# Cluster masks for routed attention: from TensorE products to VectorE writes into the scores' PSUM banks, in the last seven pairs of heads

## The chip, the cores and the metric

The kernel runs on one core of a Trainium2 chip. The metric is the device time of one execution in microseconds. The engines are TensorE (PE in the profile, its weight loads PEld), VectorE (DVE), ScalarE (ACT), GpSimd (POOL) and the queue that issues DMAs (SP). Each engine works through its own queue of instructions in order and waits for others by semaphores.

## The reference

Routed attention over 4 batches of 8 heads, 768 positions and head size 64, and behind it a feed-forward network (FFN) with hard-swish. Each query and each key is assigned to one of 16 clusters of its head, and a query sees only the keys of its own cluster:

```python
q_assign = np.argmax(np.einsum('bhsd,hcd->bhsc', q_n, c_n), axis=-1)
k_assign = np.argmax(np.einsum('bhsd,hcd->bhsc', k_n, c_n), axis=-1)
mask = q_assign[:, :, :, None] == k_assign[:, :, None, :]
scores = scale * np.matmul(q, k.transpose(0, 1, 3, 2))
scores = np.where(mask, scores, -1000000000.0)
attn = np.exp(scores - np.max(scores, axis=-1, keepdims=True))
attn = attn / (np.sum(attn, axis=-1, keepdims=True) + 1e-09)
x = np.matmul(attn, v)          # then reshaped to 3072 tokens x 512
h = x @ w_in                    # 512 -> 2048
y = (h * np.clip(h + 3.0, 0.0, 6.0) / 6.0) @ w_out
```

(q_n, k_n and c_n are the unit vectors.)

## The kernel before

Heads are worked in 16 pairs of two (t = 0, 1 in the code), g = 0 to 15. A pair has 12 steps: two halves of 384 queries (hf) times six blocks of 128 keys (j). Step n of 192 makes one tile of scores for both heads, keys on the partitions: `ps`, 128 x 2 x 384 in two PSUM banks, out of a pool of two such tiles. Per step:

- `scores`: two mask products and two score products on TensorE, summed in PSUM. The score product takes the turned q and k (`xf`, fp32, 64 rows per head; each is two instructions in the profile). The mask product takes the turned one-hot cluster vectors (`xm`, bf16, made by `route` and `route_turn`), those of the keys inverted and scaled by -2^60, so that every pair in different clusters gets a huge negative score.
- `exponentials`: ScalarE reads `ps` and writes `ex` (six buffers). This frees the `ps` tile for step n + 2.
- `key_sums`: GpSimd adds `ex` into `acc`.
- `attn_v`: TensorE multiplies `ex` with v into `pv`, six steps to a half; ScalarE copies it to `num`.
- `divide`: two products with ones turn `acc` into denominators `pd`; VectorE takes the reciprocal and multiplies `num`.

The order of all instructions is written out by hand (`manual_schedule`): the program's order is each engine's order. From step 96 on (pair 8, `DECODED`), the loop over n goes in double steps and `four_by_four` groups two of them. With r = n mod 12:

- At r = 0, 4, 8: scores of n and n + 1, exponentials, and then `attn_v` of the four steps before.
- At r = 2, 6, 10: scores of n and n + 1, exponentials, and after them FFN items out of the list `fill`, with the preparation of the next pair (`prep_items`) between them: turning q and k at r = 2, the routing at r = 6, `route_turn` at r = 10. Then the next double step's scores follow at once in TensorE's queue.

The count of FFN items per group of four steps comes from `items_by`, 53 items to 48 steps, so 4 or 5. One block of the FFN is 8 up items and 7 down items. An up item (`halved`) is 14 products in the two PSUM tiles uX and uY. VectorE works in three parts on it: a copy and two adds after uX, three adds after uY, and a clip, which `finish` defers by one item (the last up item of a block does two). A down item is 8 or 16 products, with adds on VectorE after parts 1, 3 and 6 only. `token_sums` (four adds) stand in part 4. Items of both kinds share one PSUM pool of two tiles (`psum_m`).

The kernel also holds a second way to mask, unused before, as `MASKED = NPAIR` exceeds every g: `clusters` makes cluster numbers instead of one-hot vectors, `spread` broadcasts those of the queries over the partitions by 12 products per pair, and `masks` multiplies `ex` by a comparison on VectorE after the exponential.

Of the kernel before, what the change touches and what calls it, by code (L numbers as in the profile page):

```python
# [17 lines left out]
C = 16  # L18
P = 128
# [97 lines left out]
def fast_path(ctx, tc, ok, q, k, v, centroids, moe_w_in, moe_w_out, out):  # L117
# [48 lines left out]
    counts = const.tile([P, 2, NPAIR], F32, name="counts")  # L166
    w_low = const.tile([P, 1], F32, name="w_low")

    MASKED = NPAIR
    st = {}  # L170
    later = []
    numbers = []
# [87 lines left out]
    cen = startp.tile([P, D], F32, name="cen")  # L260
    parity = const.tile([P, 2], F32, name="parity")

    number = const.tile([P, C], BF16, name="number")

    def constants():
        make_identity(nc, ident)
        for t in range(2):
            nc.vector.tensor_reduce(
                out=parity[:, t : t + 1],
                in_=ident.rearrange("p (h t c) -> p t h c", t=2, c=C)[:, t], axis=AX.XY, op=ALU.max,  # L270
            )
        nc.gpsimd.memset(half_c, 0.5)
        nc.gpsimd.memset(low_c, 1.0 / BOUND)
        nc.gpsimd.memset(ones, 1.0)
        nc.gpsimd.memset(w_low, W_LOW)
        nc.gpsimd.memset(one_hot, 0.0)
        for c in range(C):
            nc.gpsimd.memset(number[:, c : c + 1], float(c))

        warm = psum_t.tile([P, 4, P], F32, name="warm", tag="t")  # L280
        for i in range(14):
            nc.tensor.transpose(out=warm[:, i % 4], in_=ident, identity=ident)
# [47 lines left out]
    def route(g):  # L330
        cs = st.pop(("cs", g))
        pr = scratch([P, NC2, 2, C], "pr")
        for i in range(NC2 // 4):
            nc.tensor.transpose(out=pr[:, 4 * i : 4 * i + 4], in_=cs[:, i], identity=ident)
        pr = pr.rearrange("p j t c -> p (j t) c")
        mx = rtp.tile([P, 2 * NC2], F32, name="mx")
        nc.vector.reduce_max(out=mx, in_=pr, axis=AX.X)
        oh = one_hot.rearrange("p j (t c) -> p j t c", t=2)[:, :, :, 0:C]
        pr = pr.rearrange("p (j t) c -> p j t c", t=2)
        mx = mx.rearrange("p (j t) -> p j t", t=2)  # L340
        halves = [slice(0, NCH), slice(NCH, NC2)]
# [14 lines left out]

        later.append(count)
        if g >= MASKED:
            numbers.append(lambda: clusters(g))

    def route_turn(g, part):
        if part == 0:
# [11 lines left out]
        return where(n)[0] >= MASKED  # L374

    def clusters(g):
        oh = one_hot.rearrange("p j (t c) -> p j t c", t=2)[:, :, :, 0:C]
        which = rtp.tile([P, NC2, 2, C], BF16, name="which")
        nc.vector.tensor_tensor(
            out=which, in0=oh, in1=number.unsqueeze(1).unsqueeze(1).to_broadcast([P, NC2, 2, C]), op=ALU.mult  # L380
        )
        qid = st["qid"] = rtp.tile([P, NCH, 2], BF16, name="qid")
        kid = st["kid", g] = kidp.tile([P, NCH, 2], F32, name="kid")
        nc.vector.tensor_reduce(out=kid, in_=which[:, NCH:], axis=AX.X, op=ALU.add)

        nc.vector.tensor_scalar(
            out=kid, in0=kid, scalar1=-1.0, scalar2=C * (C - 1) / 2.0, op0=ALU.mult, op1=ALU.add
        )
        qsum = rtp.tile([P, NCH, 2], F32, name="qsum")
        nc.vector.tensor_reduce(out=qsum, in_=which[:, 0:NCH], axis=AX.X, op=ALU.add)  # L390
        nc.vector.tensor_copy(out=qid, in_=qsum)

    def spread(g, part):
        if part == 0:
# [14 lines left out]

    def scores_qk(n):  # L410
        st["ps", n] = psum_s.tile([P, 2, 512], F32, name="ps")
        scores_part(n, st["xf", where(n)[0]], True, by_vector(n))

    def scores_part(n, x, first, last):
        g, hf, j = where(n)
        for t in range(2):
            r = slice(t * D, (t + 1) * D)
            nc.tensor.matmul(  # L418
                st["ps", n][:, t, 0:HALF], lhsT=x[r, NCH + j],
                rhs=x[r, hf * NHC : (hf + 1) * NHC], start=first, stop=last,  # L420
            )

    def scores(n):
        g, hf, j = where(n)
        if ("ps", n) not in st:
            if hf == j == 0 or by_vector(n):
                scores_qk(n)
            else:  # L430
                st["ps", n] = psum_s.tile([P, 2, 512], F32, name="ps")
                scores_part(n, st["xm", g], True, False)
                scores_part(n, st["xf", g], False, True)
                return
        if not by_vector(n):
            scores_part(n, st["xm", g], False, True)

    def exponentials(n):
        sc = st.pop(("ps", n))[:, :, 0:HALF]
        ex = st["ex", n] = expp.tile([P, 2, HALF], F32, name="ex")  # L440
        nc.scalar.activation(out=ex, in_=sc, func=ACT.Exp, scale=SM_SCALE)  # L441

    def masks(n):
        g, hf, j = where(n)
        if not by_vector(n):
            return
        ex = st["ex", n]
        for t in range(2):
            nc.vector.scalar_tensor_tensor(
                out=ex[:, t].rearrange("p (a b) -> p a b", b=P),  # L450
                in0=st["xm", g][:, t * NCH + hf * NHC : t * NCH + (hf + 1) * NHC],
                scalar=st["kid", g][:, j, t : t + 1], in1=ex[:, t].rearrange("p (a b) -> p a b", b=P),
                op0=ALU.is_equal, op1=ALU.mult,
            )

    def key_sums(n):
# [27 lines left out]


    def divide(n):
        g, hf, _ = where(n)
# [10 lines left out]
        rcp = nump.tile([P, HALF], F32, name="rcp")  # L498
        nc.vector.reciprocal(out=rcp, in_=pd)  # L499
        nc.vector.tensor_tensor(out=num, in0=num, in1=rcp, op=ALU.mult)  # L500

        def keep():
            nc.sync.dma_start(st["xd", b][:, kt, hf * HALF : (hf + 1) * HALF], num)
            in_range(2 * g + hf, rcp)
            if (kt, hf) == (NKT - 1, 1):
                later.append(lambda: (waiting.extend((b, m) for m in range(NHC)), load_block()))

        return keep


    def in_range(i, rcp):
# [278 lines left out]

    st["early"] = st["free"] = True
    st["last"] = False
    fill, checks, unmasked = [], [], []
    st["done"], st["valued"] = 0, DECODED - lag_v

    def check_all():
# [8 lines left out]
    def four_by_four(n, r, steps):  # L805
        for i in steps:
            scores(i)
        if r % 4 == 2:
            for i in steps:
                exponentials(i)  # L810
            unmasked.extend(steps)
            check_all()
            for op in numbers:
                op()
            numbers.clear()
            return


        for i in steps[: 1 if r == 8 else 2]:
            exponentials(i)  # L820
        check_all()
        for i in unmasked:
            masks(i)
            key_sums(i)
        unmasked.clear()
        if r == 4 or n >= total:
            m = n - r % per_pair - 1 if n < total else total - 1
            if ("acc", *where(m)[:2]) in st and m < st["valued"]:
                later.append(divide(m))
                ready(m)  # L830
        for i in range(st["valued"], min(n, total)):
            attn_v(i)
            if i % per_pair == NCH - 1:
                later.append(divide(i))
        st["valued"] = min(n, total)
        for i in steps[1 if r == 8 else 2 :]:
            exponentials(i)
        for i in steps:
            masks(i)
            key_sums(i)  # L840

    with tc.manual_schedule():
        nc.scalar.dma_start(cen, centroids.rearrange("h c d -> (h c) d"))
# [17 lines left out]
        for n in range(0, total + lag_d + 2, 2):  # L861
# [25 lines left out]
            if not fours or r % 4 == 2 or n >= total:  # L887
                want = min(items_by(n + 2) - st["done"], len(fill))
                st["done"] += want
                for i in range(max(len(prep), want)):  # L890
                    if i < want:
                        fill.pop(0)()
                    if i < len(prep):
                        prep[i]()
            if r == 6 and fours:
                load(g + 2, "q", "k")
                load(g + 1, "v")
# [403 lines left out]
```

## Time and profile before

| | |
|---|---|
| time, median of 3 (lowest to highest) | 1015.35 us (1015.34 to 1015.49) |
| span of the profiled execution | 1013.6 us |
| granted TensorE clock | 0.999 |
| score products, `ps<-xf` | 768 rows, mean 487 ns, 157.1 us |
| mask products, `ps<-xm` | 384 rows, mean 327 ns, 61.0 us |
| exponentials, ACT `ex<-ps` | 192, mean 805 ns |
| reciprocal, DVE `rcp<-pd` | 32, mean 2554 ns |
| clip, DVE `g_sb<-sx,g_sb` | 88, mean 770 ns |
| turning the one-hots, PE `po` and ACT `xm<-po` | 192 of mean 220 ns, 32 of mean 806 ns |

How to read it: a row's mean is the time of one instruction from its start to its end. Matmuls are pipelined, so the mean is longer than what one adds to TensorE's queue; that has to be read as the distance from start to start in the timeline. A line of the timeline shows the start, the time until the group's end, the engine, the line, what is written and read, the shape and the count, and in brackets idle time before it with the one that ended it. The window of the last seven pairs (9 to 15) is 308 to 766 us after the span's start.

### The profile page before, as it was taken

The page shows a single profiled execution, that of the slowest core. Times are in us where ns is not written, and L with a number is a line of the kernel's source. Part 1 is how long each engine was busy: PE and PEld are TensorE (multiplying, and loading weights), DVE is VectorE, ACT ScalarE, POOL GpSimd, SP SyncE. Part 2 cuts the span into 40 slices and gives each one's busy share as a digit, 9 for nine tenths or more (in the row PEclk, how much of TensorE's full clock was granted, in tenths as well). Part 3 has the DMA queues.
Part 4 walks back from the last instruction along what each step waited for, and adds up shares of the span by engine and source line. Part 5 has one row for each costly group of instructions (what it writes and reads, how often), then busy time and mean ns, then how long its engine had stood idle before and what let it go on. Part 6 is the DMA issues. An engine that isn't in the chain of part 4 may idle for free.

```text
span 1013.6 us, 16743 instructions
## 1 busy us (share of the span) xinstructions
PE 988.4 (98%) x6560; PEld 735.4 (73%) x6560; DVE 567.6 (56%) x1085; ACT 389.6 (38%) x764; POOL 431.6 (43%) x363
## 2 busy tenths in 40 slices
PE   7999989999999999999999999999999999999996
PEld 4444445555788777788787777778777899999996
DVE  5899977868955255226236247147146372727270
ACT  6888876766233233233323333333223020201010
POOL 3776757666516326426415426515426130303030
PEclk9999999999999999999999999999999999999999
DMA  6455654523262052223323225123023041414120
GB/s 175 105 146 146 167 146 117 137 69 74 102 169 84 9 148 75 55 80 86 73 84 100 46 69 135 28 76 102 21 91 92 30 145 38 130 52 116 52 63 25
DMA packets 108041, 92.70 MB, mean 91 GB/s; under 512 B 78513, under 2 KB 88753, under 8 KB 107953
## 3 DMA queue, kind: packets, MB, share of 16 engines
q1 hardware_dynamic: 107808, 91.51, 33.1%
q8 instruction: 54, 0.88, 0.4%
q14 instruction: 35, 0.28, 0.1%
q10 hardware_dynamic: 144, 0.03, 0.0%
HBM read 75.79 MB, written 15.73 MB: 90 GB/s over the span
## 4 chain that ended last, share of the span: by engine, by line
PE 82%; DVE 2%; ACT 1%; issue 0%; ACTq 0%
PE Y L693 17%; PE uY L658 15%; PE X L693 12%; PE uX L658 12%; PE ps L418 11%; PE pv L474 9%; PE ph L613 3%; PE pd L495 2%; PE pqk L310 1%; PE pcs L323 1%; PE po L367 1%; ACT g_sb L523 0%; ACT xm L369 0%; DVE sx L669 0%; DVE g_sb L526 0%
## 5 line engine op out<-in xcount | busy, mean ns | idle before, releaser
L464 POOL TENSOR_TENSOR acc<-acc,ex 128x768 f32<-128x768 f32 x128 | 241.2, 1884 | 139.7 <-ACT ex L441 133.1
L648 POOL TENSOR_TENSOR g_sb<-g_sb 128x256 f32<-128x256 f32 x176 | 129.4, 757 | 318.0 <-DVE g_sb L526 296.8
L441 ACT ACTIVATE ex<-ps 128x768 f32<-128x768 f32 x192 | 148.4, 805 | 84.4 <-PE ps L418 83.8
L523 ACT ACTIVATE sx<-g_sb,half_c 128x512 f32<-128x512 f32 x88 | 63.6, 722 | 268.3 <-DVE g_sb L669 268.3
L418 PE MATMUL ps<-xf 64*128 64x384 f32 x768 | 157.1, 487 | 0.9 <-ACT ex L441 0.9
L474 PE MATMUL pv<-ex,vt 128*64 128x384 f32 x768 | 141.1, 496 | 0.0
L700 DVE TENSOR_TENSOR y<-y,Y 128x256 f32<-128x256 f32 x48 | 20.2, 420 | 168.1 <-PE Y L693 167.3
L474 PEld LDWEIGHTS pv<-ex,vt 128*64 128x64 f32 x768 | 48.7, 136 | 82.4 <-issue 73.8
L499 DVE RECIPROCAL rcp<-pd 128x384 f32<-128x384 f32 x32 | 81.7, 2554 | 38.7 <-PE pd L495 38.6
L461 POOL TENSOR_TENSOR acc<-ex 128x768 f32<-128x768 f32 x32 | 59.3, 1853 | 93.2 <-ACT ex L441 93.2
L658 PE MATMUL uX<-xb,w_in_sb 128*128 128x128 f32 x704 | 93.0, 275 | 0.0
L693 PE MATMUL X<-w_out_sb,g_sb 128*128 128x256 f32 x384 | 89.7, 381 | 0.0
L693 PE MATMUL Y<-T,g_sb 128*128 128x256 f32 x384 | 87.3, 380 | 0.0
L693 PE MATMUL Y<-w_out_sb,g_sb 128*128 128x256 f32 x384 | 87.2, 380 | 0.0
L658 PEld LDWEIGHTS uX<-xb,w_in_sb 128*128 128x128 f32 x704 | 85.7, 192 | 0.0
L418 PEld LDWEIGHTS ps<-xf 64*128 64x128 f32 x768 | 67.8, 188 | 21.1 <-issue 17.5
L693 PEld LDWEIGHTS X<-w_out_sb,g_sb 128*128 128x128 f32 x384 | 71.3, 190 | 12.9 <-issue 3.5
L693 PEld LDWEIGHTS Y<-T,g_sb 128*128 128x128 f32 x384 | 72.3, 190 | 11.2 <-issue 1.7
L693 PEld LDWEIGHTS Y<-w_out_sb,g_sb 128*128 128x128 f32 x384 | 72.2, 190 | 11.1 <-issue 1.1
L418 PE MATMUL ps<-xm 64*128 64x384 bf16 x384 | 61.0, 327 | 7.4 <-ACT ex L441 4.0
L526 DVE SCALAR_TENSOR_TENSOR g_sb<-sx,g_sb 128x512 f32<-128x512 f32 x88 | 67.2, 770 | 0.9 <-ACT sx L523 0.9
L669 DVE TENSOR_TENSOR g_sb<-uY,sx 128x128 f32<-128x128 f32 (+1 forms) x176 | 65.7, 414 | 0.3 <-DVE sx L669 0.2
(110 smaller groups left out, 1384.2 us busy)
## 6 DMA issues: line engine op xcount, KB each, us to landing
tx<-td SPq DMA_DIRECT2D x86, 384.0 KB, 3.3
raw<-in_moe_w_in_dram SPq DMA_DIRECT2D x16, 512.0 KB, 3.9
raw<-in_moe_w_out_dram SPq DMA_DIRECT2D x16, 512.0 KB, 3.8
qk<-in_q_dram SPq DMA_DIRECT2D x32, 192.0 KB, 4.6
qk<-in_k_dram SPq DMA_DIRECT2D x32, 192.0 KB, 4.9
vt<-in_v_dram SPq DMA_DIRECT2D x32, 192.0 KB, 4.4
xd<-num SPq DMA_DIRECT2D x32, 192.0 KB, 3.0
xb<-xd SPq DMA_DIRECT2D x12, 512.0 KB, 4.3
```

Source lines behind the costliest of these rows:

```text
L418: nc.tensor.matmul(st["ps", n][:, t, 0:HALF], lhsT=x[r, NCH + j], rhs=x[r, hf * NHC : (hf + 1) * NHC], start=first, stop=last,)
L441: nc.scalar.activation(out=ex, in_=sc, func=ACT.Exp, scale=SM_SCALE)
L461: nc.gpsimd.tensor_tensor(out=acc, in0=st["ex", n - 1], in1=ex, op=ALU.add)
L464: nc.gpsimd.tensor_tensor(out=acc, in0=acc, in1=ex, op=ALU.add)
L474: nc.tensor.matmul(pv[t * D : (t + 1) * D], lhsT=vt[:, j, t], rhs=ex[:, t], start=(j == 0), stop=(j == NCH - 1),)
L499: nc.vector.reciprocal(out=rcp, in_=pd)
L523: nc.scalar.activation(out=r, in_=h, func=ACT.Relu, bias=half_c, scale=1.0 / 6.0)
L526: nc.vector.scalar_tensor_tensor(out=g, in0=r, scalar=1.0, in1=h, op0=ALU.min, op1=ALU.mult)
L648: eng.tensor_tensor(out=out_, in0=in0, in1=in1, op=op)
L658: nc.tensor.matmul(dst, lhsT=w[:, kt], rhs=x(kt), start=(kt == 0), stop=(kt == HK - 1))
L669: nc.vector.tensor_tensor(out=out_, in0=in0, in1=in1, op=ALU.add)
L693: nc.tensor.matmul(bank[:, half * HC : (half + 1) * HC], lhsT=g_sb[:, kind, i], rhs=w[:, i], start=(first and i == 0), stop=(last and i == ...
```

## The change

From pair 9 on (`MASKED = NPAIR // 2 + 1`), masks are made by VectorE, and not on `ex` but in PSUM, ahead of the product. `masks(n)` takes the `ps` tile of step n as soon as its last reader, the exponential of step n - 2, is done, and writes into it 0 where the query's cluster number equals the key's, and -2^60 elsewhere: one TENSOR_SCALAR per head, 128 x 384, from `xm` (now bf16 cluster numbers, spread over the partitions) with the key's number as a scalar per partition. The score product then runs with `start=False` and adds to what is there. This takes the mask products of 84 steps off TensorE.

The masks are issued one double step ahead. At r = 0, 4, 8 they follow the exponentials directly, before the reciprocal, which `sum_up` splits off `divide` for that. At r = 2, 6, 10 the four masks (two steps, two heads) go into a list `singles`, and one is issued after each FFN item (at r = 6 none after the first; at r = 10 none after the first two, one after the third and up to two after each further one, since `spread` stands there); what is left follows after the loop. `clusters` is cut into three operations that come after that. Key sums, in all groups from step 96 on, are issued right after the exponentials instead of a double step later.

```diff
-    MASKED = NPAIR
+    MASKED = NPAIR // 2 + 1
...
-    def masks(n):
+    def masks(n, heads=(0, 1)):
         g, hf, j = where(n)
-        if not by_vector(n):
+        if n >= total or not by_vector(n):
             return
-        ex = st["ex", n]
-        for t in range(2):
-            nc.vector.scalar_tensor_tensor(
-                out=ex[:, t].rearrange("p (a b) -> p a b", b=P),
+        if ("ps", n) not in st:
+            st["ps", n] = psum_s.tile([P, 2, 512], F32, name="ps")
+        for t in heads:
+            nc.vector.tensor_scalar(
+                out=st["ps", n][:, t, 0:HALF].rearrange("p (a b) -> p a b", b=P),
                 in0=st["xm", g][:, t * NCH + hf * NHC : t * NCH + (hf + 1) * NHC],
-                scalar=st["kid", g][:, j, t : t + 1], in1=ex[:, t].rearrange("p (a b) -> p a b", b=P),
-                op0=ALU.is_equal, op1=ALU.mult,
+                scalar1=st["kid", g][:, 1, j, t : t + 1], scalar2=-FAR,
+                op0=ALU.not_equal, op1=ALU.mult,
             )
...
     def scores(n):
         g, hf, j = where(n)
+        if by_vector(n):
+
+            scores_part(n, st["xf", g], False, True, True)
+            return
...
         if r % 4 == 2:
             for i in steps:
                 exponentials(i)
-            unmasked.extend(steps)
+            for i in steps:
+                key_sums(i)
             check_all()
-            for op in numbers:
-                op()
-            numbers.clear()
+            for i in (n + 2, n + 3):
+                singles.extend(lambda i=i, t=t: masks(i, [t]) for t in range(2))
             return
...
         for i in steps[: 1 if r == 8 else 2]:
             exponentials(i)
         check_all()
-        for i in unmasked:
-            masks(i)
-            key_sums(i)
-        unmasked.clear()
+        for i in steps[: 1 if r == 8 else 2]:
+            masks(i + 2)
+        inverse = None
...
+        for i in steps[1 if r == 8 else 2 :]:
+            masks(i + 2)
         for i in steps:
-            masks(i)
             key_sums(i)
+        if inverse:
+            later.append(inverse())
...
                     if i < len(prep):
                         prep[i]()
+
+                    for _ in range({6: i > 0, 10: max(min(i - 1, 2), 0)}.get(r, 1)):
+                        if singles:
+                            singles.pop(0)()
+                if fours:
+                    for op in singles + numbers:
+                        op()
+                    singles.clear(), numbers.clear()
```

More of the change, by code (lines that the diff above doesn't have):

```diff
@@ L261, in fast_path @@
     parity = const.tile([P, 2], F32, name="parity")
-    number = const.tile([P, C], BF16, name="number")
+    number = const.tile([P, 2, C], BF16, name="number")
     def constants():
@@ L277, in constants @@
         for c in range(C):
-            nc.gpsimd.memset(number[:, c : c + 1], float(c))
+            nc.gpsimd.memset(number[:, 0, c : c + 1], c - C * (C - 1) / 2.0)
+            nc.gpsimd.memset(number[:, 1, c : c + 1], -float(c))
         warm = psum_t.tile([P, 4, P], F32, name="warm", tag="t")
@@ L358, in route @@
         if g >= MASKED:
-            numbers.append(lambda: clusters(g))
+            numbers.extend(clusters(g))
     def route_turn(g, part):
@@ L376, in clusters, with weigh, collect, narrow @@
     def clusters(g):
[L377 to L381, printed above, removed]
-        qid = st["qid"] = rtp.tile([P, NCH, 2], BF16, name="qid")
[L383 to L391, printed above, removed]
+        oh = one_hot.rearrange("p (h j) (t c) -> p h j t c", h=2, t=2)[:, :, :, :, 0:C]
+        which = rtp.tile([P, 2, NCH, 2, C], BF16, name="which")
+        qid = st["qid"] = rtp.tile([P, NCH, 2], BF16, name="qid")
+        kid = st["kid", g] = kidp.tile([P, 2, NCH, 2], F32, name="kid")
+        def weigh():
+            for h in range(2):
+                nc.vector.tensor_tensor(
+                    out=which[:, h], in0=oh[:, h],
+                    in1=number[:, h].unsqueeze(1).unsqueeze(1).to_broadcast([P, NCH, 2, C]), op=ALU.mult,
+                )
+        def collect():
+            nc.vector.tensor_reduce(out=kid, in_=which, axis=AX.X, op=ALU.add)
+        def narrow():
+            nc.vector.tensor_copy(out=qid, in_=kid[:, 0])
+        return [weigh, collect, narrow]
     def spread(g, part):
@@ L411, in scores_qk, with scores_part @@
         st["ps", n] = psum_s.tile([P, 2, 512], F32, name="ps")
-        scores_part(n, st["xf", where(n)[0]], True, by_vector(n))
-    def scores_part(n, x, first, last):
+        scores_part(n, st["xf", where(n)[0]], True, False)
+    def scores_part(n, x, first, last, onto=False):
         g, hf, j = where(n)
@@ L420, in scores_part @@
                 rhs=x[r, hf * NHC : (hf + 1) * NHC], start=first, stop=last,
+                skip_group_check=onto,
             )
@@ L426, in scores @@
         g, hf, j = where(n)
+        if by_vector(n):
+            scores_part(n, st["xf", g], False, True, True)
+            return
         if ("ps", n) not in st:
-            if hf == j == 0 or by_vector(n):
+            if hf == j == 0:
                 scores_qk(n)
@@ L434, in scores @@
                 return
-        if not by_vector(n):
-            scores_part(n, st["xm", g], False, True)
+        scores_part(n, st["xm", g], False, True)
     def exponentials(n):
@@ L441, in exponentials @@
         nc.scalar.activation(out=ex, in_=sc, func=ACT.Exp, scale=SM_SCALE)
-    def masks(n):
+    def masks(n, heads=(0, 1)):
         g, hf, j = where(n)
-        if not by_vector(n):
+        if n >= total or not by_vector(n):
             return
-        ex = st["ex", n]
-        for t in range(2):
-            nc.vector.scalar_tensor_tensor(
-                out=ex[:, t].rearrange("p (a b) -> p a b", b=P),
+        if ("ps", n) not in st:
[3 more added lines that the diff above has]
+                out=st["ps", n][:, t, 0:HALF].rearrange("p (a b) -> p a b", b=P),
                 in0=st["xm", g][:, t * NCH + hf * NHC : t * NCH + (hf + 1) * NHC],
-                scalar=st["kid", g][:, j, t : t + 1], in1=ex[:, t].rearrange("p (a b) -> p a b", b=P),
-                op0=ALU.is_equal, op1=ALU.mult,
+                scalar1=st["kid", g][:, 1, j, t : t + 1], scalar2=-FAR,
+                op0=ALU.not_equal, op1=ALU.mult,
             )
@@ L486, in divide, with sum_up @@
     def divide(n):
+        return sum_up(n)()
+    def sum_up(n):
         g, hf, _ = where(n)
@@ L497, in divide, with inverse, keep @@
             )
[L498 to L508, printed above, removed]
+        def inverse():
+            rcp = nump.tile([P, HALF], F32, name="rcp")
+            nc.vector.reciprocal(out=rcp, in_=pd)
+            nc.vector.tensor_tensor(out=num, in0=num, in1=rcp, op=ALU.mult)
+            def keep():
+                nc.sync.dma_start(st["xd", b][:, kt, hf * HALF : (hf + 1) * HALF], num)
+                in_range(2 * g + hf, rcp)
+                if (kt, hf) == (NKT - 1, 1):
+                    later.append(lambda: (waiting.extend((b, m) for m in range(NHC)), load_block()))
+            return keep
+        return inverse
     def in_range(i, rcp):
@@ L792, in fast_path @@
     st["last"] = False
-    fill, checks, unmasked = [], [], []
+    fill, checks, singles = [], [], []
     st["done"], st["valued"] = 0, DECODED - lag_v
@@ L828, in four_by_four @@
             if ("acc", *where(m)[:2]) in st and m < st["valued"]:
-                later.append(divide(m))
+                inverse = sum_up(m)
                 ready(m)
@@ L833, in four_by_four @@
             if i % per_pair == NCH - 1:
-                later.append(divide(i))
+                inverse = sum_up(i)
         st["valued"] = min(n, total)
```

## The prediction

> **What bounds the kernel now.** I read the busy shares first, then the chain of waits, then a window over the seven pairs that change (308 to 766 us, found from the rows of `ps` in the timeline), and last the timelines of TensorE and VectorE around single joints.
>
> ```profile
> PE 988.4 (98%) x6560; PEld 735.4 (73%) x6560; DVE 567.6 (56%) x1085; ACT 389.6 (38%) x764; POOL 431.6 (43%) x363
> PE 82%; DVE 2%; ACT 1%; issue 0%; ACTq 0%
> 308.00:766.00 458.00, 456.93 (x3098) 350.24 (x3097) 198.42 (x436) 150.01 (x269) 196.36 (x166) 1.00 0.28 74
> PE uX L658 <- DVE sx L669: 1.1, 3, 0.5
> ```
>
> The third line is the window: length, then busy time of PE, PEld, DVE, ACT and POOL, clock, DMA. TensorE is busy 456.93 of 458.00 us; the fourth line, the only wait of TensorE there, is 1.1 us. So each microsecond taken off TensorE in this window shortens the kernel, and each that TensorE newly waits lengthens it. VectorE has 198.42 us of work (43%).
>
> **What the Trainium skill says.** "TensorE: Matmul & The Clock Gate", section "Wait — 56ns, not 53.3ns?", has warm matmuls start N / 2.4 GHz + 2.5 ns apart: 162.5 ns for 384 columns. The trace agrees: four fp32 instructions of one score product take 0.64 to 0.65 us. "PSUM — Partial Sum Buffer", section "Engine vs sequencer instructions", has the other queues in strict order and matmuls starting in program order; nothing in the trace contradicts it, so a matmul that waits for a mask holds all behind it. "VectorE: DVE Perf Modes", section "Why PSUM operands drop a tier", denies the two-port mode to an operation that touches PSUM and gives fp32 there one element per cycle; the 128x512 TENSOR_SCALAR into PSUM takes 695 ns, the same as the three-operand form (696), which fits.
>
> **Removed: the mask products.** One double step now:
>
> ```profile
> 627.42 0.34 PE L418 MATMUL ps<-xm 64*128 64x384 bf16 x2
> 627.60 0.81 PE L418 MATMUL ps<-xf 64*128 64x384 f32 x4
> 628.24 0.33 PE L418 MATMUL ps<-xm 64*128 64x384 bf16 x2
> 628.40 0.81 PE L418 MATMUL ps<-xf 64*128 64x384 f32 x4
> 629.14 1.51 PE L474 MATMUL pv<-ex,vt 128*64 128x384 f32 x8
> ```
>
> From start to start, a pair of mask products costs 0.17 us, not the 327 ns of its row: the two heads overlap. The double step lasts 629.14 - 627.42 = 1.72 us. Without masks it is 2 x 0.65 + 0.09 for the hand-over = 1.39 us, or 1.49 if the first product starts as where a pair begins with `xf`:
>
> ```profile
> 311.51 0.92 PE L418 MATMUL ps<-xf 64*128 64x384 f32 x4
> 312.26 0.49 PE L418 MATMUL ps<-xm 64*128 64x384 bf16 x4
> ```
>
> (0.75 us to the next). 42 double steps change; 7 of them begin a pair and last 1.81 us now. The gain is 35 x 0.23 + 7 x 0.32 = 10.3 us to 35 x 0.33 + 7 x 0.42 = 14.5 us; I take **-12.5**.
>
> Spread for route_turn: 12 transposes (six in 0.34 us) give way to 12 bf16 products of the same shape: nothing. ScalarE evicts 3 x 0.56 (as the `xf` copies of that shape) instead of 2 x 0.81 us: nothing, with 150 of 458 us busy. The `clusters` work, about 1.4 us of VectorE per pair (two products near 0.35, a reduction near 0.55, a copy), comes after the loop at r = 6 and is wanted at r = 10: nothing. Key sums start sooner on POOL (196 of 458 us busy): nothing.
>
> **Added: 168 masks on VectorE.** No such row exists. Nearest:
>
> ```profile
> L225 DVE TENSOR_SCALAR wtop<-raw x32: 683/695/714, 12.2 to 228.7; 128x512 uint32<-128x512 uint32 x32
> ```
>
> Same operation, SBUF to PSUM, 512 elements in 0.695 us. At 0.96 elements per ns (the 0.96 GHz of the VectorE page's specifications), 128 fewer are 0.133 less: 0.56 us, which also matches the 0.547 of `g_sb<-uY,sx` 128x384 (mean over all its rows). Bounds: 0.36 if bf16 input gave two elements per cycle, 0.69 if nothing scaled. 168 x 0.56 = 94 us brings VectorE to some 300 of 458 us. That is no bound by itself. Position is what counts.
>
> **Added wait 1: at r = 0, 4, 8 (new masks before attn_v).** Exp of step n ends about 2.5 us after the scores start, two masks take 1.1, the next two follow the second exp; TensorE has pd and four attn_v, 2.7 to 3.4 us after its own 1.4. At worst some tenths: hidden by attn_v.
>
> **Added wait 2: at the joint from the FFN items to the next scores.** At r = 2, 6, 10 the four masks are issued one after each FFN item, each behind that item's own VectorE work, and the scores are the next thing in TensorE's queue. What VectorE does when the last item was an up item, with the scores starting at 602.85:
>
> ```profile
> 602.95 0.29 DVE L669 TENSOR_TENSOR sx<-uY,sx 128x128 f32<-128x128 f32 x1 [0.85 <-PE uY L658]
> 603.16 0.75 DVE L669 TENSOR_TENSOR g_sb<-uY,sx 128x128 f32<-128x128 f32 x2
> 603.82 0.68 DVE L526 SCALAR_TENSOR_TENSOR g_sb<-sx,g_sb 128x512 f32<-128x512 f32 x1
> ```
>
> These three groups need the item's last product, so they begin only when the scores begin, and end f = 1.65 us later. A mask behind them starts 0.08 before that end (as 603.82 against 603.91) and takes 0.56; TensorE follows 0.05 later (after the wait on sx at 617.73 it starts at 617.78). The last mask is there at f + 0.53; each further one left over adds 0.48. TensorE wants the last at about 1.0 (three heads of 0.325). Stall: f - 0.47, plus 0.48 for each mask more.
>
> The count of items per block of four steps, 53 per 48 steps, is 4 or 5; with `{6: i > 0, 10: max(min(i - 1, 2), 0)}` this fixes what is left behind the last item. By the start of the scores, with f read from VectorE's timeline:
>
> - ordinary up item, one left: 311.5, 535.4, 602.9, 694.9; f = 2.04, 1.66, 1.65, 1.89: 5.4 us
> - up item, three left: 378.3, 445.2 (2.10, 1.66), two left: 759.3 (2.09): 6.8 us
> - last up item of a block, with two clips, one left: 398.6, 627.4 (2.60, 2.63): 4.3 us
> - first up item, no clip pending, one left: 515.1, 670.5 (1.06 each): 1.2 us
> - down item ending in adds: one left at 332.5, 357.9 (0.93, 0.98), three at 649.2, 716.0 (0.98, 0.93): 3.9 us
> - masks all given out earlier, or no adds in the last item: 424.0, 468.6, 490.2, 557.0, 582.2, 739.7: 0
>
> Together **+21.5** over 21 joints, or 16.7 with masks of 0.36 and 24.7 with 0.69 us.
>
> **Added wait 3: VectorE between up items.** An up item takes 3.15 us of TensorE, and VectorE idles 0.56 to 1.1 us in each, so one mask fits. Two in an item (r = 10), and the reciprocal (2.56 us, then num, 1.14 in this window), which now goes behind the masks and so starts about 1.5 us later before the FFN items at r = 8, free a uX bank late: some 0.7 us in three pairs plus a few tenths elsewhere: **+2.5** (0 to 5).
>
> Sum: 1015.35 - 12.5 + 21.5 + 2.5 = 1026.9, say **1027 us**. The price is paid because a short PE job leaves for a queue whose newest work depends on TensorE's own last products.
>
> **Rivals.**
>
> - *Hidden masks, faster.* VectorE has half its time free, and six of my 21 joints already show no wait. If the remaining masks are in the banks in time as well, only the gain and wait 3 stay: 1015.35 - 12.5 + 2 = 1005 us. Against it is the order of VectorE's queue.
> - *Break-even.* Masks at 0.36, a full gain and no wait 3: 1015.35 - 14.5 + 16.7 = 1017.5; a few joints shorter than I read, and it is 1015.
> - *VectorE becomes the bound of the up stretches.* Clips on VectorE already stretch from 0.68 to 1.1 us where POOL works. If masks stretch alike, to 1.1 us, the joints cost 21.5 + 24 x 0.54 = 34.5 (24 masks left over in all) and wait 3 doubles: 1042 us. Against it: a mask has one SBUF operand, the clip two.
>
> **How the numbers follow.** My forecast 0.60 (1018 to 1034), hidden masks 0.20 (1000 to 1012), break-even 0.10, VectorE bound 0.10. The range 1007 to 1036 keeps the first, the third and edges of the other two, about 0.8. Faster: 0.20 + 0.05 of break-even = 0.25; same 0.04; slower 0.71.
>
> **What would show it.** The list of waits should have PE `ps` on the mask line near 20 us in some 15 pieces of 0.5 to 2.6, none at the six joints named; the PE rows of `ps<-xm` should fall from 384 to 216; a double step without a stall should last 1.4 to 1.5 us; the mask row should show about 0.56 us. I am wrong if PE waits there sum to less than 12 us, which would mean that the masks stand earlier in VectorE's queue than I read in the loop, or if the mask row is far from 0.56.

## The result and the profile after

The changed kernel takes **1042.88 us** (median of 4 runs, 1042.68 to 1043.1) against 1015.42 us for the kernel before on the same chip: ratio **1.0265**, 95% interval 1.0247 to 1.0282. It is slower, as forecast, but by 27.5 us where 11.6 were forecast, and the time lies above the range.

The first lines of the page after, engine shares and the chain's shares, and below them the window from the first score product of pair 9 to the end of the last double step of pair 15, now 312 to 792.9 us (its columns as before: length; busy time of PE, PEld, DVE, ACT, POOL; clock; DMA share; GB/s):

```profile
PE 991.5 (95%) x6392; PEld 731.2 (70%) x6392; DVE 666.5 (64%) x1281; ACT 389.9 (37%) x771; POOL 431.7 (41%) x379
PE 75%; DVE 8%; ACT 2%; issue 1%; DMA 0%; SPq 0%; ACTq 0%
312.00:792.90 480.90, 454.63 (x2897) 341.53 (x2898) 291.91 (x619) 149.35 (x273) 191.01 (x163) 0.99 0.26 70
```

VectorE's part of the chain that ended last has grown from 2% to 8%. In the window TensorE is idle for 480.90 - 454.63 = 26.3 us where it was idle for 1.07. But it is also busy for about as long as before (456.93), though 168 mask products are gone, and its clock stands at 0.99. So there are two losses: waiting, and a busy time that did not fall. The waits of TensorE in that window, and the group of masks on VectorE:

```profile
PE ps L424 <- DVE ps L460: 23.9, 18, 2.4
PE uX L676 <- DVE sx L687: 0.5, 3, 0.2
L460 DVE TENSOR_SCALAR ps<-xm,kid x168: 603/619/624, 307.2 to 791.4; 128x384 f32<-128x384 bf16 x168
L424 PE MATMUL ps<-xm x216: 319/323/333, 14.9 to 294.4; 64*128 64x384 bf16 x108
```

A wait line holds the sum, how often and the longest. The masks are all but the only thing that TensorE waits for. Their own time hardly varies: 603 to 624 ns in 168 of them. The last line says where mask products are left: none after 294.4 us.

**A double step with no stall**, a joint where all masks were given out earlier, in TensorE's timeline:

```profile
480.87 1.56 PE L424 MATMUL ps<-xf 64*128 64x384 f32 x8
482.36 0.87 PE L509 MATMUL pd<-acc,ones 128*64 128x384 f32 x4
```

It lasts 482.36 - 480.87 = 1.49 us. **A joint with one mask left** behind an ordinary up item, the one of before at 535.37; TensorE, then VectorE:

```profile
548.48 0.92 PE L424 MATMUL ps<-xf 64*128 64x384 f32 x4
550.73 0.92 PE L424 MATMUL ps<-xf 64*128 64x384 f32 x4 [1.33 <-DVE ps L460]
551.57 0.87 PE L509 MATMUL pd<-acc,ones 128*64 128x384 f32 x4
```

```profile
549.46 0.68 DVE L544 SCALAR_TENSOR_TENSOR g_sb<-sx,g_sb 128x512 f32<-128x512 f32 x1
550.05 0.62 DVE L460 TENSOR_SCALAR ps<-xm,kid 128x384 f32<-128x384 bf16 x1
```

The mask stands behind the clip of the last up item, ends at 550.67, and TensorE goes on at 550.73. The double step takes 551.57 - 548.48 = 3.09 us, a stall of 3.09 - 1.49 = 1.60. "Stall" below is always this difference, and where TensorE waits before the first product of the double step, that wait is added.

**A joint with three masks left**, the worst, and TensorE by stretches of 2 us around it:

```profile
384.65 2.93 PE L424 MATMUL ps<-xf 64*128 64x384 f32 x8 [2.36 <-DVE ps L460]
387.51 3.03 PE L485 MATMUL pv<-ex,vt 128*64 128x384 f32 x16
```

```profile
382.00:384.00 2.00, 0.29 (x3) 0.10 (x1) 1.67 (x5) 0.62 (x1) 1.52 (x3) 1.00 0.53 123
384.00:386.00 2.00, 1.35 (x4) 0.68 (x6) 1.74 (x4) 0.10 (x1) 0.00 (x0) 0.65 0.19 74
386.00:388.00 2.00, 2.00 (x8) 0.73 (x8) 0.72 (x2) 1.18 (x2) 0.00 (x0) 0.50 0.00 0
388.00:390.00 2.00, 2.00 (x14) 0.84 (x12) 1.72 (x3) 0.44 (x1) 1.48 (x1) 1.00 0.00 0
```

Seventh number of each row: after the wait of 2.36 us the granted clock drops to half for 3.4 us (in slices of 0.1 us, from 384.61 to 388.02). The products after the wait take 2.86 us from their start to the next product instead of 1.49; part of that is still waiting for masks. The same happens after waits of 2.17 us (456.43), of 2.36 us (786) and of 1.45 and 0.26 us (738), for 3.4 us each time; in the rest of the window the clock is 1.00.

From the first score product to the end of the last double step, 454.77 us have become 481.49. The account of these 26.7 us, from the two timelines:

| | forecast | measured |
|---|---|---|
| shorter double steps (mask products gone) | -12.5 | -10.1 |
| stalls at 21 joints | +21.5 | +31.1 |
| attn_v at half clock | 0 | +2.9 |
| double steps off the joints, FFN items | +2.5 | +2.8 |
| sum | +11.5 | +26.7 |

### The profile page after: what moved, and what is told of

Read it like the earlier page. It is cut to its first block, busy times and chain, and to the rows that moved or that the text cites. A ratio compares the mean times of both kernels' runs of the same rounds, so it can differ in the third digit from the quotient of the medians.

```text
span 1041.2 us, 16660 instructions
## 1 busy us (share of the span) xinstructions
PE 991.5 (95%) x6392; PEld 731.2 (70%) x6392; DVE 666.5 (64%) x1281; ACT 389.9 (37%) x771; POOL 431.7 (41%) x379
## 4 chain that ended last, share of the span: by engine, by line
PE 75%; DVE 8%; ACT 2%; issue 1%; DMA 0%; SPq 0%; ACTq 0%
PE Y L711 16%; PE uY L676 14%; PE X L711 12%; PE uX L676 11%; PE ps L424 8%; PE pv L485 8%; PE ph L631 3%; DVE ps L460 2%; PE pd L509 1%; PE pqk L311 1%; DVE g_sb L687 1%; DVE g_sb L544 1%; DVE rcp L515 1%; PE pcs L324 1%; DVE sx L687 1%
## 5 line engine op out<-in xcount | busy, mean ns | idle before, releaser
L424 PE MATMUL ps<-xf 64*128 64x384 f32 x768 | 161.5, 510 | 24.7 <-DVE ps L460 23.9
L485 PE MATMUL pv<-ex,vt 128*64 128x384 f32 x768 | 143.6, 503 | 0.0
L460 DVE TENSOR_SCALAR ps<-xm,kid 128x384 f32<-128x384 bf16 x168 | 101.8, 617 | 30.7 <-ACT ex L451 28.8
```

The lines of the kernel that those rows point to most:

```text
L424: nc.tensor.matmul(st["ps", n][:, t, 0:HALF], lhsT=x[r, NCH + j], rhs=x[r, hf * NHC : (hf + 1) * NHC], start=first, stop=last, skip_group_ ...
L460: nc.vector.tensor_scalar(out=st["ps", n][:, t, 0:HALF].rearrange("p (a b) -> p a b", b=P), in0=st["xm", g][:, t * NCH + hf * NHC : t * NC ...
L485: nc.tensor.matmul(pv[t * D : (t + 1) * D], lhsT=vt[:, j, t], rhs=ex[:, t], start=(j == 0), stop=(j == NCH - 1),)
```

## The experiments

**Theory A:** the price comes from the place of the last masks, behind VectorE's work on the last FFN item; take them out of that place and the joints are free. **Rival B:** the price comes from VectorE's load (94 us more at the forecast size), and would follow the masks wherever they go. Beside them stands the half clock as a cost of its own.

### e1_ahead: masks before the FFN items instead of after them

```diff
-            for i in (n + 2, n + 3):
-                singles.extend(lambda i=i, t=t: masks(i, [t]) for t in range(2))
+            order = [(i, t) for t in range(2) for i in (n + 2, n + 3)]
+            singles.extend(lambda i=i, t=t: masks(i, [t]) for i, t in (order if r == 10 else sorted(order)))
...
                 for i in range(max(len(prep), want)):
+                    for _ in range({10: (0, 1, 1, 2, 0)[i]}.get(r, 1)):
+                        if singles:
+                            singles.pop(0)()
                     if i < want:
                         fill.pop(0)()
...
-                    for _ in range({6: i > 0, 10: max(min(i - 1, 2), 0)}.get(r, 1)):
```

At r = 10 the order among the four masks changes too: the first heads of both steps come ahead of the second heads.

> The changed kernel with one thing moved: at r = 2, 6 and 10 each mask is issued before its FFN item instead of after it, so none is left behind the last item. Theory A (what costs is the place of the last masks in VectorE's queue, behind adds that wait for TensorE's last products): the waits of the score products for masks at the joints, 23.9 us now, fall below 3 us, the half clock goes, and the mask-free double steps keep their 0.23 us: 1015.4 - 10.3 + 2 to 4 us for late uX banks and reciprocals = 1007 to 1009 us. Rival B (VectorE has too much work, 100 us more, wherever it stands): the same work stands in the same stretches, the waits move to uX and stay near 20 us: 1030 to 1043 us.

Measured: 1025.66 us, ratio 1.010 (1.007 to 1.013). Neither figure. All 21 joints now last 1.49 us: the stalls are gone, as A says. But other waits stand in their place:

```profile
PE pcs L324 <- DVE rcp L515: 6.1, 6, 1.1
PE uX L676 <- DVE sx L687: 4.1, 6, 0.9
PE ps L424 <- DVE ps L460: 3.8, 6, 1.7
```

```profile
545.31 1.56 PE L424 MATMUL ps<-xf 64*128 64x384 f32 x8
548.01 0.85 PE L324 MATMUL pcs<-xf,cnT 128*32 128x384 f32 x8 [1.15 <-DVE rcp L515]
```

The cluster products `pcs` of the next pair share their one PSUM tile with the denominators `pd`, which the reciprocal reads; the masks went ahead of that reciprocal. Against the kernel without masks below, the same window is 16.1 us longer: 9.6 in double steps off the joints (6.5 of it where the six waits for the reciprocal stand: five of them cost 1.2 us each, one 0.5), 2.8 around attn_v, 3.7 among FFN items. Of the 2.8, 1.8 stand at one place, where two tiny operations run between masks of pair 14:

```profile
704.70 1.59 DVE L395 CAST qid<-kid 128x12 bf16<-128x12 f32 x1
706.21 0.61 DVE L460 TENSOR_SCALAR ps<-xm,kid 128x384 f32<-128x384 bf16 x1
706.74 1.52 DVE L953 TENSOR_SCALAR alone<-counts 128x16 f32<-128x16 f32 x1
708.18 0.61 DVE L460 TENSOR_SCALAR ps<-xm,kid 128x384 f32<-128x384 bf16 x1
708.70 0.16 DVE L953 TENSOR_SCALAR alone<-counts 128x16 f32<-128x16 f32 x1
```

The same `alone` operation takes 1.52 us at 706.74 and 0.16 at 708.70. Two adds of GpSimd run in this stretch; they end at 706.27 and 708.23, and the two long operations end within 0.03 us of them.

### e2_nomasks: the gain by itself

```diff
         if by_vector(n):
-            scores_part(n, st["xf", g], False, True, True)
+            st["ps", n] = psum_s.tile([P, 2, 512], F32, name="ps")
+            scores_part(n, st["xf", g], True, True)
             return
...
     def masks(n, heads=(0, 1)):
-        if n >= total or not by_vector(n):
-            return
+        return
```

> The changed kernel without the masks: the 168 VectorE writes are left out, and the score products of the last seven pairs start their sums afresh, so these pairs attend without clusters. Everything else of the change stays. Theory A: TensorE has no wait at the joints, double steps of 1.49 us instead of 1.72 (1.81): 1015.4 - 10.3 = 1005 us, up to 1007 with the later reciprocal. If the gain was as I first took it (12.5): 1003 us. Rival C (the product onto written PSUM, spread, clusters or the moved key sums cost the time, not the masks): over 1020 us.

Measured: 1010.42 us, ratio 0.9937 (0.9916 to 0.9958): rival C fell, but the time is 3 us above the figure. Its window:

```profile
311.80:757.90 446.10, 445.26 (x2912) 342.26 (x2911) 204.29 (x456) 147.84 (x275) 192.15 (x164) 1.00 0.28 76
```

All 42 double steps last 1.49 us, and from first score product to the last double step's end it takes 444.64 us, 10.1 less than before. That is the whole gain the change can have in this window. The timed runs show 6.1 us of it (1016.53 us for the kernel before on that chip). In the profile, the stretch ahead of the window is 1.6 us longer than before (313.1 against 311.5), and is so already at the first `ph` product (145.40 against 143.81 us), ahead of every step that the change touches; the stretch behind it is 0.7 us longer (248.0 against 247.3). Why wasn't followed.

### e3_order: the new order without the new masks

```diff
-    MASKED = NPAIR // 2 + 1
+    MASKED = NPAIR
```

> The changed kernel with MASKED back at 16: all pairs take the mask products on TensorE, and of the change only the order remains (key sums right after the exponentials, the reciprocal behind them). Theory A: within 1.5 us of the kernel before, 1015 to 1017 us; the pcs products may wait for a late reciprocal, about 1 us. Rival D (the moved key sums or reciprocals make a good part of the 27.5 us): 1020 us or more.

Measured: 1016.91 us, ratio 0.9997 (0.9985 to 1.0009), as expected. Earlier key sums and the reciprocal cut off from `divide` cost nothing.

### e4_warm and e8_warm_all: TensorE kept busy while it waits

```diff
+    def keep_busy(count):
+        warm = psum_t.tile([P, 4, P], F32, name="warm", tag="t")
+        for i in range(count):
+            nc.tensor.transpose(out=warm[:, i % 4], in_=ident, identity=ident)
...
         for i in steps:
+            if i - DECODED in IDLE:
+                keep_busy(IDLE[i - DECODED])
             scores(i)
```

e4_warm puts 12 transposes ahead of the scores at the five longest waits; e8_warm_all puts 11 to 20 into each of the eleven waits over 1.2 us. Both leave every mask where the changed kernel has it.

> The changed kernel with 12 transposes of the identity (1.3 us of TensorE) put into the five longest waits for masks, those after which the clock fell to half or might (the joints with three or two masks left). Theory A (a wait of over two microseconds costs again, by half clock in the products after it): the clock stays at 1.00 and these joints get 4 to 6 us shorter in all though TensorE has more work: 1037 to 1039 us. Rival E (the slow products after the wait have another cause, and the granted clock doesn't follow from idleness): 1043 us or more.

Measured: 1041.7 us, ratio 1.0251 (1.0233 to 1.0269): above the figure of A and below that of E, a miss. The four filled joints that had had the half clock now kept the full one and, with the attn_v behind them, became 1.0 to 1.6 us shorter; the fifth (667.66) had not had it and stayed as long. But now the half clock followed an unfilled wait of 2.27 us that had gone free in the changed kernel (the clock of 2 us slices after it):

```profile
409.42 1.14 PE L424 MATMUL ps<-xf 64*128 64x384 f32 x4 [2.27 <-DVE ps L460]
```

```profile
409.00:411.00 2.00, 1.58 (x6) 0.59 (x8) 1.51 (x3) 0.34 (x1) 1.92 (x3) 0.75 0.11 38
411.00:413.00 2.00, 2.00 (x8) 0.71 (x6) 1.47 (x3) 0.47 (x1) 2.00 (x3) 0.50 0.00 0
```

So where it strikes depends on more than the length of the wait. e8_warm_all therefore fills all the long waits.

> The changed kernel with transposes of the identity in all eleven waits for masks of over 1.2 us, 11 to 20 in each (1.2 to 2.2 us), since in e4_warm, with five of them filled, the half clock showed after a sixth. Theory A (half clock follows the idle time): no stretch of the joints has a clock below 1.00, attn_v after them takes as long as before, 1037 to 1039 us. Rival E (the clock falls for another reason): 1041 us or more, with half clock still there.

Measured: 1037.67 us, ratio 1.0216 (1.0188 to 1.0244), clock 0.998, as A says; up to the last product no stretch of 2 us has a clock below 1.00. (One of the four timed runs took 1042.04 us at a clock of 0.996; no trace of it was kept.) The joint with three masks again:

```profile
381.30 2.35 PE L826 MATMUL warm<-ident 128*128 128x128 f32 x20
383.84 0.92 PE L424 MATMUL ps<-xf 64*128 64x384 f32 x4 [0.19 <-DVE ps L460]
385.01 0.92 PE L424 MATMUL ps<-xf 64*128 64x384 f32 x4 [0.26 <-DVE ps L460]
385.86 2.80 PE L485 MATMUL pv<-ex,vt 128*64 128x384 f32 x16
```

The masks come no sooner, but the products behind them run at full speed, and so does attn_v (2.80 against 3.03 us). From the first score product to the last double step's end it takes 475.48 us against 481.49: 3.0 us less in attn_v, 2.1 inside the joints, and 0.9 among FFN items, most of it a wait for a DMA that the changed kernel had. So the half clock costs about 5 us.

**When the clock falls** can be read from the trace of the changed kernel. In slices of 0.1 us it falls at 384.61, 456.29, 739.59 and 787.38 us, and once more, after the last product, at 1036.55. The distances are 71.68, 283.30, 47.79 and 249.17 us: 21, 83, 14 and 73 times 3.413 us, and 3.41 us is also how long each of the first four spells lasts. So in this trace the clock changes only at points of a fixed grid of 3.413 us. Between these points, TensorE was idle as follows:

| grid step, us | TensorE idle in it | clock in the next step |
|---|---|---|
| 381.19 to 384.61 | 2.31 | 0.50 |
| 452.87 to 456.29 | 2.02 | 0.50 |
| 736.18 to 739.59 | 1.71 | 0.50 |
| 783.97 to 787.38 | 2.15 | 0.50 |
| 312.93 to 316.34 | 1.69 | 1.00 |
| 405.09 to 408.50 | 1.61 | 1.00 |
| e4_warm, 406.57 to 409.98 | 2.27 | 0.50 |

In the changed kernel, every step with 1.71 us of idle time or more (half of the step) was followed by the half clock, and none with 1.69 or less. The wait of 2.27 us at 405.98 lies across two steps (1.61 and 0.66 us) and went free; in e4_warm the same wait lies within one. The limit is not that sharp in all runs: a step with 1.82 us idle near 144 us of e4_warm went free, and one with 1.38 us in e10_heads was followed by the half clock.

### e5_pcs, e6_best, e7_hole, e9_split: the waits of e1_ahead taken away in turn

e5_pcs is e1_ahead with the cluster products one FFN item later, so that they no longer wait for the reciprocal:

```diff
-            if prep and r == (6 if fours else 4):
+            if prep and r == 4 and not fours:
                 prep.pop(0)()
```

> As e1_ahead, and the next pair's cluster products (pcs, at r = 6) stand one FFN item later. In e1_ahead the joints cost nothing any more (double steps of 1.49 us), but TensorE waited six times 1.2 us before pcs, whose PSUM tile is the one that the late reciprocal still reads; e1_ahead is 16 us behind e2_nomasks over the 21 blocks, 7.2 of it there. Theory A2 (a second wait, hidden in the changed kernel behind the joints, is the reciprocal's place behind the masks): these waits go, e1_ahead minus 5 to 7 us: 1018 to 1021 us on this chip. Rival (VectorE's sheer work; the wait only moves to uX): no change, 1024 to 1026 us.

Measured: 1020.68 us, ratio 1.0045 (1.0035 to 1.0055). As expected in time. The six waits are gone, and the window is 11.9 us behind the kernel without masks instead of 16.1: 5.7 us less in double steps off the joints, 1.5 more among FFN items. So a part of the waits did move on.

e6_best also moves the kernel's closing tests of its totals (`good`, `fit`, `alone`) from between masks of pair 14 to ahead of the last FFN items.

> As e5_pcs, and the small checks of the totals at the end of the program are put behind the last attention step instead of where the scheduler had put them, between two masks of pair 14 (there they held up masks by about 3.8 us in e1_ahead). Theory A2: e5_pcs minus 3 to 4 us: 1014 to 1017 us, level with the kernel before or just below. Rival: as e5_pcs.

Measured: 1023.36 us, ratio 1.0061 (1.004 to 1.0083): a miss, above both figures. The window shrank by 3.1 us, but the transpose of these tests now stands in TensorE's queue with the last FFN items behind it, and waits for VectorE's chain:

```profile
PE pl L956 <- DVE one L954: 2.1, 1, 2.1
```

That is half of the 4.2 us by which the stretch behind the window grew against e5_pcs; the other half, and 3.3 us ahead of the window, were not followed.

e7_hole puts each mask inside its FFN item: in an up item into VectorE's idle time between the adds on uX and those on uY, in a down item at its start:

```diff
             add(sx[:, 2], X[:, 2], sx[:, 0])
+            spend()
             Y = psum_m.tile([P, 4, P], F32, name="uY", tag="m")
```

> As e6_best, but each mask stands inside its FFN item: in an up item between the adds on uX and those on uY, where VectorE idles 0.56 to 0.85 us for uY in the kernel before; in a down item at its start. Theory A: the masks at the joints are as early as in e6_best, and the adds on uX are no later than before, so the waits of uX go: e6_best minus 1 to 3 us, 1011 to 1015 us. Rival B: no better than e6_best.

Measured: 1018.2 us, ratio 1.0007 (0.9995 to 1.002). Five us better than e6_best, but above the figure: its window is 5.3 us below that of before, and the work outside takes that back, with the same wait of 2.1 us behind the window. e9_split keeps the masks of e7_hole and cuts the closing tests in two, VectorE's part after the ninth of the last FFN items, TensorE's after the twelfth.

> As e7_hole, with the small checks of the totals in two pieces among the last FFN items (VectorE's part after the ninth item, the transpose and the rest after the twelfth). In e7_hole the 21 blocks are 5.3 us shorter than in the kernel before, but the stretch after them is 5 us longer, with a wait of 2.1 us for those checks. Theory A: that goes, e7_hole minus 3 to 5 us: 0.994 to 0.998 of the kernel before, the first version faster than it. Rival: the time after the blocks has another cause, and it stays at 1.000.

Measured: 1015.41 us against 1017.36 us for the kernel before on this chip, ratio **0.9977** (0.9967 to 0.9987), as expected: the only version here that computes everything and is faster than both kernels, if only by 0.2%. Its window and its waits for masks there:

```profile
314.10:764.05 449.95, 447.28 (x2900) 340.58 (x2899) 295.08 (x613) 149.30 (x274) 192.00 (x163) 1.00 0.28 75
PE ps L424 <- DVE ps L460: 1.0, 3, 0.4
```

VectorE does 295 us of work in it, as much as in the changed kernel (291.91), and TensorE waits 1.0 us for masks instead of 23.9. **This decides against B:** the same load in another order costs almost no wait. The window is 4.8 us shorter than that of before, out of 10.1 possible. The single profiled executions of the two do not show the gain (both span 1013.6 us): this one is 2.6 us longer ahead of the window, where it has a spell of half clock from 144 us on that the profile of the kernel before lacks, far ahead of the steps that the change touches; and it is 2.2 us longer behind the window, 1.7 of it after the last product. The 0.23% rests on the timed runs.

### e10_heads: one score tile per head

```diff
-        st["ps", n] = psum_s.tile([P, 2, 512], F32, name="ps")
+        st["ps", n] = [psum_s.tile([P, 512], F32, name=f"ps{t}") for t in range(2)]
```

(and one exponential per head.) The idea was that the first head's product need not wait for the second head's mask.

> The changed kernel with one score tile per head in place of one for both (two exponentials of 384 per step in place of one of 768). In the changed kernel both heads' products start after both masks; I think that this, not a longer mask, made the stalled joints about 0.41 us longer than I worked out. Theory A: with a tile for each head the first head's product of the second step starts at once and only the second waits: stalled double steps with one mask left get 0.3 to 0.4 us shorter (3.09 to about 2.75 us where the last item is an ordinary up item). Rival F (the mask's end reaches TensorE later than I took it): no shorter. The total isn't comparable, as ScalarE has more to do in the first half.

Measured: 1043.34 us, ratio 1.0256 (1.0218 to 1.0294): the joints with one mask left are no shorter. The one of above again, and another, which took 3.37 us in the changed kernel:

```profile
551.57 1.55 PE L424 MATMUL ps<-xf 64*128 64x384 f32 x6
553.82 0.91 PE L424 MATMUL ps<-xf 64*128 64x384 f32 x2 [0.69 <-ACT ex L452]
554.66 0.87 PE L510 MATMUL pd<-acc,ones 128*64 128x384 f32 x4
```

```profile
719.47 1.55 PE L424 MATMUL ps<-xf 64*128 64x384 f32 x6
721.99 0.91 PE L424 MATMUL ps<-xf 64*128 64x384 f32 x2 [0.97 <-DVE ps L461]
722.83 1.51 PE L486 MATMUL pv<-ex,vt 128*64 128x384 f32 x8
```

The first head does start at once (6 instructions before the wait, not 4). But the remaining head alone takes 554.66 - 553.82 = 0.84 us to the next product, just what both heads took in the changed kernel (551.57 - 550.73 = 0.84). (Here the profile names an exponential of ScalarE as what ended the wait; it ends together with the mask, at 553.77. At 721.99 it names the mask, and the rest is the same 0.84.) Nothing is saved by starting one early, because the two run side by side. The Trainium skill, "TensorE: Matmul & The Clock Gate", section "The mechanism" under "Packing small matmuls — row/col tiling", has matmuls on different row groups of the array run at the same time; the 0.84 us for one head and for two agree.

## Why the prediction was half right

**Right: the mechanism and its places.** The masks trail behind the last FFN item and TensorE's next work stands behind them. The joints by the prediction's own groups, stalls in us:

| joints | forecast | measured |
|---|---|---|
| ordinary up item, one left (4) | 5.4 | 7.05 |
| up item, two or three left (3) | 6.8 | 10.05 |
| last up item of a block, two clips (2) | 4.3 | 5.1 |
| first up item (2) | 1.2 | 2.0 |
| down item ending in adds (4) | 3.9 | 6.6 |
| the six named as zero | 0 | 0.26 |

Five of the six are zero, and the sixth is 0.26. e1_ahead removes all the stalls by moving the masks alone.

**Right: what was costed at nothing**, by e3_order for the order, and by e2_nomasks for the spread and the clusters, which it keeps. And wait 3, +2.5 forecast, measured 2.8: 1.9 in double steps off the joints (1.2 of it one wait of `pcs` for a late reciprocal), 0.9 among FFN items, of which 0.7 is a wait for a DMA.

**Wrong: "TensorE wants the last at about 1.0 (three heads of 0.325)".** The prediction itself had read that the two heads of the mask products overlap, and then priced the score products as if one head were half of two. e10_heads shows that one head takes as long as both, so the last mask is wanted when the second step starts, at 0.65 us. The same slip is in its reading of "four fp32 instructions of one score product" as four times 162.5 ns one after the other: the sum came out right by luck, for two of the four take the same 0.65 us alone. With the mask at 0.617 us instead of the 0.56 that was estimated, this makes 0.35 + 0.06 = 0.41 us for each of the 15 stalled joints, about 6.1 us; each of them did measure at least 0.39 above its forecast.

**Wrong: no term for the clock.** The prediction costed the wait and not what follows it. In the changed kernel half clock adds 2.9 us to attn_v, and e8_warm_all shows 2.1 more inside joints. This is also about half of why TensorE's busy time did not fall: it is 9.4 us above that of e2_nomasks. The other half comes from the waits themselves, since a product with a wait behind it shows its full 0.92 us as busy where otherwise the next one starts after 0.65. The Trainium skill, "TensorE: Matmul & The Clock Gate", section "What's actually happening", gives half rate after at least one idle window of about 3.4 us. The length of the window agrees with the grid of 3.413 us; but 1.71 us of idle time in it sufficed, so the measurement decides, and the page's figure would not have warned of these waits.

**Mis-sized: the gain**, taken as 12.5 in the middle of 10.3 to 14.5. The double step became 1.49 us, the one of the two readings that came from a trace line (a pair that begins with `xf`); the 1.39 was argued. That is 2.4 us.

**Mis-sized: each further mask**, priced at 0.48. Three masks in a row take 1.79 us, so each further one adds 0.59; for the nine further ones that is 1.0 us. With 0.3 us at a joint that was named as zero (557.0), the account of the stalls is 6.1 + 2.1 (half clock) + 1.0 + 0.3 = 9.5 us, by which they exceed the forecast.

**The rivals.** *Hidden masks* fell: 15 of 21 joints stall by 0.87 us or more. *Break-even* fell with all its conditions: masks at 0.36, a full gain, no wait 3. *VectorE bound* named 1042, and the kernel took 1042.88, but its mechanism isn't there: no mask exceeds 624 ns, waits for uX are 1.0 us in the whole span as against 1.1 before, and e9_split runs with the same VectorE work faster than before. A time that fits proves no cause.

**Open.** Where the limit for the half clock lies in general: it is near half of a grid step in the changed kernel, and other runs have exceptions. Nor were the 5.3 us settled that e9_split's window still lacks to the kernel without masks: 2.6 of it stand in double steps off the joints, 2.3 among FFN items, 0.4 around attn_v.

## What to carry to other kernels

Work handed to an idle engine is priced by its place in that engine's queue: find what stands ahead of it, when that ends, and which queue stops for it. The same 168 masks cost 31 us of stalls behind the last item's adds, and 1.0 us of waits for masks in the holes between adds (5.3 us in all against no masks). Moving one wait can uncover the next (here a reciprocal that held a shared PSUM tile), so give a forecast of such a repair a range up to the next wait. And cost a wait of TensorE of about 1.7 us or more at its length plus a possible spell at half clock, here about 1.2 us for each of four.

## What the runs showed of the hardware

- In the changed kernel the clock fell to 0.50 only at points of a grid of 3.413 us, for 3.41 us each time within the work, and only where TensorE had been idle for 1.71 us or more of the grid step before (1.69 went free). A wait of 2.27 us that lay across two steps cost nothing more, one that lay within a step did.
- A fp32 score product on 64 rows takes TensorE as long alone as with the other head's beside it (0.84 us to the next product in both cases); start to start it is 0.65 us.
- Tiny VectorE operations from and to SBUF can take ten times their usual time: 1.52 us instead of 0.16. GpSimd's adds were running in that stretch and ended within 0.03 us of the stretched operations; that these are the cause was not tried. The masks, which write PSUM, never stretched (603 to 625 ns in every kept trace).
